# A fused attention and feed-forward kernel: the hand-written issue order runs on to step 27, and the last pair of f blocks is staged whole

## The chip, the core and the metric

The kernel runs on one core of a Trainium2 chip, in one launch. The time is device microseconds (us) of that core, the median of several executions. The engines named below are PE (TensorE: matmul, with its weight loads counted apart as PEld), DVE (VectorE), ACT (ScalarE), POOL (GpSimd) and SP (SyncE, which here only issues DMAs). Each engine has a list of instructions of its own, and in the trace they start in the order of that list.

## What is computed

```python
# q, k, v: (8, 8, 576, 64)   factor = 4
q_d, k_d, v_d = (a.reshape(B, H, S // 4, 4, D).mean(axis=3) for a in (q, k, v))
out_up = np.repeat(softmax_attn(q_d, k_d, v_d), 4, axis=2)      # down-sampled attention
scores = np.where(abs(pos[:, None] - pos[None, :]) < 4, scale * q @ k.T, -1e9)
out_local = softmax(scores) @ v                                 # band of 7 diagonals
x = (out_up + out_local).transpose(0, 2, 1, 3).reshape(4608, 512)
h = np.maximum(x @ w_in, 0)                                     # w_in 512 x 2048
out = (s * h * h + b) @ w_out                                   # w_out 2048 x 512
```

## The kernel before

**Feed-forward.** The 4608 tokens are cut into 18 blocks `t` of 256, the 2048 hidden features into 8 pairs `p` of 128-wide f blocks. One *step* is one (t, p). Its first product ("G", line 622, buffer `ph`) is 24 matmuls of 256 columns: x and w_in are each held as a high and a low part, and three of the four cross products are summed. ACT then does relu, square and a cast (`upper`, "R", lines 635 to 637, `gh`), DVE the low part `gl` (`lower`, "V", line 642). The second product ("H", lines 684 to 686, `po`) is 12 matmuls of 512 columns that sum over all p of a block; its first two thirds need `gh`, each third matmul needs `gl`. After p = 7 DVE scales the sum and adds the bias (line 696), and SP sends it out. The list `order` gives the steps: in both kernels the first 24 steps cover the blocks 0, 1 and 2 for all p, and step 24 is (3, 0).

**Weights.** The weights arrive as 64-bit floats. A pair's two halves (w_in part and w_out part) are loaded into a staging buffer (`load_w`, line 223), and `convert` (lines 247 to 257) makes the high and low parts: a chunk takes an ACT scaling, four DVE operations, an ACT cast and a DVE subtraction. Pairs 0 to 6 go through whole staging buffers of 1 MB a half. Pair 7 has no staging buffer: `load_quarter` (line 232) brings it in eight quarters of 256 columns through the two small buffers `pv`, and the same two buffers hold `convert`'s intermediate `es`.

**Bias.** The term b @ w_out is the column sum of w_out times b: `add_rows` adds 31 pieces on DVE (line 658), `column_sums` multiplies by ones on PE (line 662) and scales on DVE (line 663).

**Attention.** A unit is one batch and one pair of heads. Units 0 to 11 (batches 0 to 2) use a banded form in three streams: `d` (down-sampled: lines 315 to 375), `v` (values, POOL: lines 300 to 305) and `l` (the band: score products 431, sums 437 to 455, the diagonal blocks 459, output products `ol` 469, sum into x 473). Batches 3 to 7 use a form in which POOL and DVE make the band (lines 527 to 549) and PE only transposes the result (`ot`, line 559).

**What sets the order.** `PLAN` is a text of stream names: `d3` is the next piece of unit 3's d stream, `c5` the next piece of weight chunk 5, `x`/`y` the split of x for blocks 0, 1 and for block 2, `G R V H` the next piece of a step. Each piece is issued when its name comes up, and every PE, DVE, ACT and POOL instruction of it is tied behind the one before it on its engine. Before, `PLAN` holds units 0 to 7, pairs 0 to 6 and steps 0 to 14 (G) or 13 (H). What follows is written out by the loop at line 864 and placed by a scheduler: pair 7 (`split_w`), the bias sums, units 8 to 11, the evictions and steps 14 on. DMAs stand in SP's own queue in the order that the scheduler gives them.

Of the kernel before, what the change touches and what calls it, by code (L numbers as in the profile page):

```python
# [11 lines left out]
F32 = mybir.dt.float32  # L12
# [7 lines left out]
P = 128  # L20
# [57 lines left out]
def attention_ffn_kernel(ctx, tc, qk, vw_in, vr_in, vdm, qkn, vn, w_in, w_out, s_in, b_in, out):  # L78
# [55 lines left out]
    def load_pair(b, hp):  # L134
        if (b, hp) not in ld:
            load_parts(b, hp, ("qk", "vr", "vd") + (("vw",) if HP * b + hp < EU else ()))
# [81 lines left out]
    def load_w(p):  # L218

        parts = (("i", src_i[:, :, 512 * p : 512 * p + 512]), ("o", src_o[:, 2 * p : 2 * p + 2]))  # L220
        for op, src in parts:
            st = one.tile([P, 1024, 2], I32, tag=f"w{op}{STAGE[p]}", name="wst")
            nc.sync.dma_start(st.rearrange("p (k f) t -> p k (f t)", k=src.shape[1]), src)
            wst[(p, op)] = st

    def load_quarter(p, op, i):
        if op == "i":
            src = src_i[:, i, 512 * p : 512 * p + 512]
        else:
# [29 lines left out]
    def split_w(p):  # L259
        for chunk in split_parts(p):  # L260
            for _ in chunk:
                pass

    def split_parts(p):
        wi[p] = one.tile([P, 2, NK, 256], F32R, tag=f"wi{p}", name="wi")
        wo[p] = one.tile([P, 2, 2, DM], F32R, tag=f"wo{p}", name="wo")
        for op, w in (("i", wi[p]), ("o", wo[p])):
            fl = w.rearrange("p s k f -> p s (k f)")
            if p < len(STAGE):
                st = wst.pop((p, op))  # L270
# [672 lines left out]
```

## Time and profile before

| | |
|---|---|
| time, median of 3 runs | 965.31 us (965.13 to 965.32) |
| the profiled execution | 966.4 us, of which its instructions span 964.6 us |
| PE, PEld | 927.1 and 834.0 us busy, 96% and 86% of the span |
| DVE, ACT, POOL | 643.9, 479.1 and 404.3 us busy |
| DMA | 86.25 MB |

A matmul's bar in the trace also covers its way through the array, so bars of neighbours overlap: two bars of 0.28 us may start 0.12 us apart. A window of the trace ("A:B") gives, for each engine, the time in which at least one of its instructions ran. The chain of waits follows the work that ended last back to its start.

### The profile page before, as it was taken

Reading aid. Unit: us, or ns where it says so; the run is one execution under the profiler, and the core shown is the slowest. Engines: PE = TensorE matmul, PEld = TensorE weight load, DVE = VectorE, ACT = ScalarE, POOL = GpSimd, SP = SyncE. Lnnn points to the kernel's source line nnn. Section 1 sums busy time; section 2 is a strip of 40 time slices with the busy share of each in tenths; the row PEclk is TensorE's granted clock in tenths of the full one; section 3 lists DMA queues with packets and bytes.
Section 4 is the critical chain, followed back from the end, with each engine's and each line's share of the span. In section 5 each row is a group of like instructions: output and inputs, shape, how many; then the busy total and the mean of one; then the engine's idle time right before and its main releaser. Section 6 shows DMA issues by size and latency. Waiting matters only on the chain.

```text
span 964.6 us, 18495 instructions
## 1 busy us (share of the span) xinstructions
PE 927.1 (96%) x7316; PEld 834.0 (86%) x7316; DVE 643.9 (67%) x1154; ACT 479.1 (50%) x1141; POOL 404.3 (42%) x440
## 2 busy tenths in 40 slices
PE   5699999979999999999999999999999999999998
PEld 4589788768999999998898899999999999999997
DVE  7999978864577878787777878787878521111121
ACT  7877785454663454544353545454536333233231
POOL 5400220100176686768678777877676200000000
PEclk9799999999999999999999999999999999999999
DMA  9745321313143232322232424142412000000000
GB/s 326 255 162 182 120 87 41 98 60 107 58 138 110 79 125 79 125 75 91 79 119 66 138 66 138 67 138 66 138 54 76 1 22 1 24 1 22 1 23 22
DMA packets 32102, 86.25 MB, mean 89 GB/s; under 512 B 3344, under 2 KB 7952, under 8 KB 32016
## 3 DMA queue, kind: packets, MB, share of 16 engines
q1 hardware_dynamic: 32016, 85.08, 26.5%
q8 instruction: 57, 0.93, 0.4%
q14 instruction: 29, 0.24, 0.1%
HBM read 75.63 MB, written 9.44 MB: 88 GB/s over the span
## 4 chain that ended last, share of the span: by engine, by line
PE 72%; DVE 14%; POOL 4%; DMA 4%; issue 3%; ACT 2%; DVEq 0%; POOLq 0%; SPq 0%; ACTq 0%
PE ph L622 33%; PE po L684 11%; PE po L685 11%; PE po L686 11%; POOL pr L527 2%; POOL acc L549 2%; PE sa L334 2%; DMA tqk<-in_qk_dram 2%; DVE es L252 1%; DMA wst<-in_moe_w_out_dram 1%; DMA lqk<-in_qkn_dram 1%; DVE es L253 1%; PE sl L431 1%; PE up L375 1%; DVE st L529 1%
## 5 line engine op out<-in xcount | busy, mean ns | idle before, releaser
L622 PE MATMUL ph<-xh,wi 128*128 128x256 f32 x2176 | 409.6, 282 | 2.4 <-DVE gl L642 1.3
L622 PEld LDWEIGHTS ph<-xh,wi 128*128 128x128 f32 x2176 | 342.2, 189 | 9.8 <-DVE gb L642 2.3
L622 PE MATMUL ph<-xl,wi 128*128 128x256 f32 x1152 | 323.4, 281 | 1.0 <-DVE xl L744 1.0
L527 POOL TENSOR_TENSOR pr<-lqk 128x576 f32<-128x576 f32 x140 | 200.5, 1455 | 74.0 <-DMA lqk<-in_qkn_dram 37.6
L622 PEld LDWEIGHTS ph<-xl,wi 128*128 128x128 f32 x1152 | 217.0, 188 | 5.7 <-DVE xl L744 1.2
L635 ACT ACTIVATE ph<-ph 128x512 f32<-128x512 f32 x144 | 83.8, 582 | 230.3 <-PE ph L622 222.1
L684 PE MATMUL po<-wo,gh 128*128 128x512 f32 x456 | 181.4, 398 | 2.4 <-ACT gh L637 2.4
L685 PE MATMUL po<-wo,gh 128*128 128x512 f32 x456 | 180.8, 396 | 0.0
L686 PE MATMUL po<-wo,gl 128*128 128x512 f32 x456 | 177.5, 395 | 0.5 <-DVE gl L642 0.5
L642 DVE TENSOR_TENSOR gl<-ph,gh 128x512 fp32r<-128x512 f32 x114 | 78.0, 684 | 116.3 <-ACT gh L637 116.2
L549 POOL TENSOR_TENSOR acc<-acc,pv 128x576 f32<-128x576 f32 x80 | 114.9, 1436 | 55.0 <-DVE acc L549 29.4
L529 DVE TENSOR_REDUCE st<-pr 128x9 f32<-128x576 f32 x140 | 106.0, 757 | 38.1 <-POOL pr L527 35.6
L686 PEld LDWEIGHTS po<-wo,gl 128*128 128x128 f32 x456 | 85.8, 188 | 18.7 <-DVE gl L642 1.0
L684 PEld LDWEIGHTS po<-wo,gh 128*128 128x128 f32 x456 | 85.9, 188 | 18.5 <-ACT gh L637 3.2
L548 DVE TENSOR_TENSOR pv<-lv,st 128x576 f32<-128x576 f32 x120 | 87.6, 748 | 19.2 <-POOL acc L549 18.8
L685 PEld LDWEIGHTS po<-wo,gh 128*128 128x128 f32 x456 | 86.0, 189 | 14.8
L637 ACT CAST gh<-ph 128x512 fp32r<-128x512 f32 x114 | 66.9, 587 | 63.1 <-PE po L685 60.2
L636 ACT ACTIVATE ph<-ph 128x512 f32<-128x512 f32 x144 | 83.7, 582 | 3.4
L305 POOL TENSOR_TENSOR dq<-vq 64x64 f32<-64x64 f32 x58 | 19.6, 337 | 123.8 <-PE up L373 121.6
L304 POOL TENSOR_TENSOR dq<-vt 80x64 f32<-80x64 f32 x58 | 18.5, 330 | 88.9 <-PE up L375 87.1
L685 PE MATMUL po<-wo,gb 128*128 128x512 f32 x120 | 46.9, 391 | 0.0
L686 PE MATMUL po<-wo,gb 128*128 128x512 f32 x120 | 46.8, 390 | 0.0
(153 smaller groups left out, 1195.3 us busy)
## 6 DMA issues: line engine op xcount, KB each, us to landing
tqk<-in_qk_dram SPq DMA_DIRECT2D x30, 584.0 KB, 4.2
lqk<-in_qkn_dram SPq DMA_DIRECT2D x20, 768.0 KB, 4.2
lv<-in_vn_dram SPq DMA_DIRECT2D x20, 480.0 KB, 3.4
out_dram<-os SPq DMA_DIRECT2D x17, 512.0 KB, 3.1
wst<-in_moe_w_in_dram SPq DMA_DIRECT2D x7, 1024.0 KB, 5.4
wst<-in_moe_w_out_dram SPq DMA_DIRECT2D x7, 1024.0 KB, 5.2
tvd<-in_vdm_dram SPq DMA_DIRECT2D x29, 160.0 KB, 2.9
tvr<-in_vr_dram SPq DMA_DIRECT2D x29, 128.0 KB, 2.5
```

The lines of the kernel that those rows point to most:

```text
L527: nc.gpsimd.tensor_tensor(pr, lqk[:, 0:CH], lqk[:, CH + o : 2 * CH + o], ALU.mult)
L529: nc.vector.tensor_reduce(ls[:, :, o], pr, AX.X, ALU.add)
L548: nc.vector.tensor_tensor(pv, lv[:, o : o + CH], w, ALU.mult)
L549: (nc.vector if o % 3 == 1 else nc.gpsimd).tensor_tensor(acc[:, :, h], acc[:, :, h], pv, ALU.add)
L622: nc.tensor.matmul(ph[:, j], wi[p][:, s, k, f], xk[:, k], start=k == 0 and s == 0 and xk is xh, stop=k == NK - 1 and s == 1)
L635: nc.scalar.activation(ph, ph, AF.Relu)
L636: nc.scalar.activation(ph, ph, AF.Square)
L637: nc.scalar.copy(gh, ph)
L642: nc.vector.tensor_tensor(gl, acc.pop((t, p)), gh.bitcast(F32), ALU.subtract)
L684: nc.tensor.matmul(po[m], gh[:, j, ms], wo[p][:, 0, j], start=first, stop=False)
L685: nc.tensor.matmul(po[m], gh[:, j, ms], wo[p][:, 1, j], start=False, stop=False)
L686: nc.tensor.matmul(po[m], gl[:, j, ms], wo[p][:, 0, j], start=False, stop=last)
```

## The change

`PLAN` is rewritten from its first piece and now reaches through step 27. It holds units 0 to 11, all eight pairs, the bias sums (`b`, `s`), the evictions of blocks 0 and 1 (`E`), the split of x for block 3 (`z`), and, as names with `w` and `q`, the places of the loads of pairs 2 to 7 and of the attention inputs of the units 5 to 11.

Pair 7 is loaded in two whole halves, one after the other, into the memory of batch 2's x, which is free until unit 8 writes there, and converted in four chunks of 512 columns. The steps of blocks 0 and 1 for pair 7 move from places 21 and 22 to places 16 and 17. Blocks 0 and 1 are evicted through buffers of the tag `xh`, which hold the split x of blocks 0 and 1 before and of block 3 after. Units 8 to 11 use the banks 2 and 3 that the sums of block 1 leave, and G alternates between bank 4 and another.

```diff
 PLAN = (
-    "d0 l0 d1 l1 d1 d2 l2 d1 l1 d2 d3 d0 d2 d1 d3 l0 l1 d1 v2 d2 d0 d2 l1 l2 d1 l1 v1 l3 d1 "
+    "d0 d0 l1 d1 l0 l1 d1 d2 d1 d3 d2 l1 d1 d3 d0 v1 l1 l0 l1 d1 l1 l0 d0 d1 l1 l2 d1 l0 d0 "
...
-    def load_w(p):
-        parts = (("i", src_i[:, :, 512 * p : 512 * p + 512]), ("o", src_o[:, 2 * p : 2 * p + 2]))
...
-    def load_quarter(p, op, i):
...
+    def load_w(p, op):
+        if op == "i":
+            src = src_i[:, :, 512 * p : 512 * p + 512]
+        else:
+            src = src_o[:, 2 * p : 2 * p + 2]
+        if p < len(STAGE):
             st = one.tile([P, 1024, 2], I32, tag=f"w{op}{STAGE[p]}", name="wst")
+        else:
+            st = new_x(2).rearrange("p h s -> p (h s)")[:, 0:2048].bitcast(I32)
+            st = st.rearrange("p (f t) -> p f t", t=2)
...
+            n = 1024 if WIDE <= p < len(STAGE) else 512
+            for j in range(0, 1024, n):
+                js = slice(j, j + n)
+                yield convert(wst[p, op][:, js], fl[:, 0, js], fl[:, 1, js], op, p)
...
-        at = 6 if t >= 3 and p % 2 else 7 if t == 1 and p < HF else 4
+        at = 4 if order.index((t, p)) % 2 == 0 else 6 if t >= 3 and (t, p) != (3, 1) else 7 if t == 1 and p < HF else 5
...
+    def evict(t):
+        if t < 2:
+            os_ = two.tile([P, 2, DM], F32, tag="xh", name="os")
+        else:
+            os_ = one.tile([P, 2, DM], F32, tag="os", name="os")
...
+    def fourth_x():
+        xs[3] = xh, xl = tuple(
+            two.tile([P, HP, TB], F32R, tag=tag, name=tag) for tag in ("xh", "xl"))
...
-    order += [(2, p) for p in range(HF)]
-    order += [(t, p) for p in range(HF, NFP) for t in range(3)]
+    order += [(2, 0), (2, 1)] + [(t, HF) for t in range(2)]
+    order += [(2, p) for p in range(2, NFP)]
...
+    bk = {0: banks(*range(8)), 1: two_banks(5, 6), 2: two_banks(2, 3)}
...
+            for name in plan:
+                if name[0] in "wq":
+                    load(name)
+                    continue
+                if name not in streams:
+                    begin_stream(name)
                 next(streams[name], None)
...
-    begin = 2 * HF
+    begin = 28
```

On DVE the first step's `gl` (line 642 before, 637 now) stands after this piece of the order. `xl` is the low part of x, `es` and `wi` belong to the weight chunks, `sm`, `pl`, `qd`, `kd`, `dmx` to attention. Before:

```order
L744 TENSOR_TENSOR xl<-x,xh 128x256
L315 TENSOR_REDUCE qd<-tqk 128x144
L317 TENSOR_REDUCE kd<-tqk 128x144
L437 TENSOR_REDUCE sm<-sl_816 128x6
L438 TENSOR_TENSOR pl<-sl_816,sm 128x192
L257 TENSOR_TENSOR wi<-es,wi 128x512
L249 TENSOR_SCALAR es<-es 128x512
L250 TENSOR_SCALAR es<-es 128x512
L642 TENSOR_TENSOR gl<-ph,gh 128x512
```

Now, from the same split of x on:

```order
L747 TENSOR_TENSOR xl<-x,xh 128x256
L308 TENSOR_REDUCE qd<-tqk 128x144
L310 TENSOR_REDUCE kd<-tqk 128x144
L254 TENSOR_SCALAR es<-es 128x512
L255 TENSOR_SCALAR es<-es 128x512
L257 SCALAR_TENSOR_TENSOR es<-wst,es 128x512
L258 SCALAR_TENSOR_TENSOR es<-wst,es 128x512
L339 RECIPROCAL dsm<-dsm 96x3
L254 TENSOR_SCALAR es<-es 128x1024
L255 TENSOR_SCALAR es<-es 128x1024
L637 TENSOR_TENSOR gl<-ph,gh 128x512
```

More of the weight chunks stands ahead of the first `gl`, a wide chunk of pair 2 (128x1024) among it; in all DVE has 114 instructions ahead of it now, and 106 before.

SP's queue around pair 7 read so before (`wst` is a quarter of pair 7; `tqk`, `tvr`, `tvd`, `tvw` are a unit's inputs):

```order
L131 DMA tvw<-in_vw_dram 128x768
L232 DMA wst<-in_moe_w_in_dram 128x512 x2
L131 DMA tqk<-in_qk_dram 128x1168
L232 DMA wst<-in_moe_w_in_dram 128x512
L131 DMA tvr<-in_vr_dram 128x256
L232 DMA wst<-in_moe_w_out_dram 128x512
L131 DMA tvd<-in_vdm_dram 80x512
L131 DMA tvw<-in_vw_dram 128x768
L232 DMA wst<-in_moe_w_out_dram 128x512 x3
L131 DMA tqk<-in_qk_dram 128x1168
```

Now the two halves of pair 7 (`x`) stand with one unit input between them, and ahead of the outputs of blocks 0 and 1:

```order
L140 DMA tvw<-in_vw_dram 128x768
L140 DMA tvd<-in_vdm_dram 80x512
L140 DMA tvr<-in_vr_dram 128x256
L237 DMA x<-in_moe_w_in_dram 128x4x512
L140 DMA tvw<-in_vw_dram 128x768
L237 DMA x<-in_moe_w_out_dram 128x2x1024
L671 DMA out_dram<-os 128x2x512 x2
L140 DMA tqk<-in_qk_dram 128x1168 x2
```

The quarters are gone from between the inputs, and no attention input stands behind four of them any more.

On ACT the split of x for block 3 (`xh`) stood among pair 7's chunks before:

```order
L247 ACTIVATE es<-wst 128x256
L442 ACTIVATE pl<-pl 128x384
L365 COPY ptm<-tp 80x288
L635 ACTIVATE ph<-ph 128x512
L603 CAST xh<-x 128x1024
L255 CAST wo<-es 128x256
L636 ACTIVATE ph<-ph 128x512
L459 COPY db<-pt 32x12x32 x4
L368 COPY ptr<-tr 64x144 x2
```

Now it stands behind the R of step 18, in unit 8's d stream (`dq`, `dmx`, `pd`, `dsm`) and ahead of the R of step 19:

```order
L632 CAST gh<-ph 128x512
L315 COPY dq<-qd 64x3x48 x2
L765 CAST xh<-x 128x1024
L331 ACTIVATE dmx<-dmx 96x3
L333 ACTIVATE pd,dsm<-sa,dmx 96x144 x3
L337 ACTIVATE dsm<-dsm,eps 96x3
L630 ACTIVATE ph<-ph 128x512
L631 ACTIVATE ph<-ph 128x512
L632 CAST gh<-ph 128x512
L342 ACTIVATE pd<-pd,dsm 96x144 x3
```

Its memory is the buffer from which block 0 has just been sent out, so it also follows the end of that transfer.

More of the change, by code (lines that the diff above doesn't have):

```diff
@@ L435, in near @@
                 yield
+                if h == 0:
+                    pl = own["pl"] if own else two.tile([P, 2 * NG, 32], F32, tag="pl", name="pl")
+                    sm = own["sm"] if own else two.tile([P, 2, 2 * NG], F32, tag="sm", name="sm")
+                    lmx, lsm = sm[:, 0], sm[:, 1]
                 hg = slice(h * NG, h * NG + NG)
@@ L649, in gemm1, with add_rows @@
             lower(t, p)
-    def add_rows(p):
-        parts = [wo[p][:, i // 2, i % 2].bitcast(F32) for i in range(4)]
-        if p == 0:
-            nc.vector.tensor_tensor(bias, parts.pop(), parts.pop(), ALU.add)
-        for part in parts:
-            nc.vector.tensor_tensor(bias, bias, part, ALU.add)
+    def add_rows():
+        for p in range(NFP):
+            parts = [wo[p][:, i // 2, i % 2].bitcast(F32) for i in range(4)]
+            if p == 0:
+                nc.vector.tensor_tensor(bias, parts.pop(), parts.pop(), ALU.add)
+                yield
+            for part in parts:
+                nc.vector.tensor_tensor(bias, bias, part, ALU.add)
+                yield
     def column_sums():
@@ L662, in column_sums @@
         nc.tensor.matmul(cs, ones, bias, start=True, stop=True)
+        yield
         nc.vector.tensor_scalar(bias, cs, sb_b, None, ALU.mult)
+        yield
+    def evict(t):
[3 more added lines that the diff above has]
+            os_ = one.tile([P, 2, DM], F32, tag="os", name="os")
+        for i in range(2):
+            nc.vector.scalar_tensor_tensor(
+                os_[:, i], oacc[t][i], sb_s, bias, ALU.mult, ALU.add)
+        nc.sync.dma_start(
+            out[TB * t : TB * t + TB, :].rearrange("(m p) c -> p m c", p=P), os_)
     def gemm2(t, p):
@@ L677, in products2 @@
         end = t == NB - 1 and p == NFP - 1
-        os_ = one.tile([P, 2, DM], F32, tag="os", name="os") if p == NFP - 1 else None
+        os_ = one.tile([P, 2, DM], F32, tag="os", name="os") if end else None
         for m in range(2):
@@ L693, in products2 @@
                     nc.sync.dma_start(out[r0 : r0 + P, cs], os_[:, m, cs])
-            elif p == NFP - 1 and m == 1:
-                for i in range(2):
-                    nc.vector.scalar_tensor_tensor(
-                        os_[:, i], po[i], sb_s, bias, ALU.mult, ALU.add)
-                nc.sync.dma_start(
-                    out[TB * t : TB * t + TB, :].rearrange("(m p) c -> p m c", p=P), os_)
+            elif p == NFP - 1 and m == 1 and t >= 2:
+                evict(t)
             yield
@@ L779, in attention_ffn_kernel, with two_banks @@
     offset_mask()
[L781 to L797 removed]
+    at = {"sa": 0, "tp": 0, "up": 0, "tr": 1, "sl0": 1, "sl1": 0, "ol": 1}
+    def two_banks(*ids):
+        return lambda shape, name: bank(ids[at[name]], shape, name)
+    bk = {0: banks(*range(8)), 1: two_banks(5, 6), 2: two_banks(2, 3)}
+    chunks = (chunk for p in range(NFP) for chunk in split_parts(p))
+    streams = {"x": begin_x(), "y": third_x(), "z": fourth_x(), "b": add_rows()}
+    streams["s"] = column_sums()
+    streams["E"] = (evict(t) for t in range(2))
     streams["G"] = (None for t, p in order for _ in products1(t, p))
@@ L801, in attention_ffn_kernel, with begin_stream, load @@
     streams["H"] = (None for t, p in order for _ in products2(t, p))
+    def begin_stream(name):
+        if name[0] == "c":
+            streams[name] = next(chunks)
+            return
+        b, hp = units[int(name[1:])]
+        for kind, steps in banded(b, hp, bk[b]).items():
+            streams[f"{kind}{HP * b + hp}"] = steps
+    def load(name):
+        if name[0] == "w":
+            load_w(int(name[1]), name[2])
+        else:
+            load_parts(*units[int(name[1:-1])], {"k": ("qk",), "v": ("vr", "vd"), "w": ("vw",)}[name[-1]])
     plan = PLAN.split()
@@ L832, in attention_ffn_kernel @@
     free = [0, 0, 16] + [((S * (b - 1) - 1) // TB) * NFP - 2 for b in range(3, B)]
-    rings = {1: banks(5, 6), 2: banks(5), 3: banks(2, 3, 5)}
+    ring = banks(2, 3, 5)
+    part_done = [i for i in range(2 * HP, EU) if f"d{i}" in streams]
     def attention_rest():
-        for i in range(2 * HP, EU):
+        for i in part_done:
+            b, hp = units[i]
+            load_pair(b, hp)
+            d, v, l = (streams[f"{kind}{i}"] for kind in "dvl")
+            next(v, None)
+            for _ in itertools.chain(d, l):
+                yield
+        for i in range(part_done[-1] + 1, EU):
             load_ahead(i)
-            yield from first_unit(*units[i], rings[min(i // HP + i // (EU - 2), 3)])
+            yield from first_unit(*units[i], ring)
         for b, g in GROUPS:
-            yield from two_pairs(b, g, rings[3])
+            yield from two_pairs(b, g, ring)
     gen = attention_rest()
-    done = NY[1]
+    done = NY[1] + NY[2] * len(part_done) // HP
     pend = []
```

72 lines of the change are left out of this document (17 added, 55 removed), and 35 rows, old and new, of the table PLAN.

## The prediction, made before the run

> **What bounds the kernel now.** I read the page's busy line, then windows of the trace, then the chain of waits in the one window that shows a loss.
>
> ```profile
> PE 927.1 (96%) x7316; PEld 834.0 (86%) x7316; DVE 643.9 (67%) x1154; ACT 479.1 (50%) x1141; POOL 404.3 (42%) x440
> 0.00:56.54 56.54, 36.02 (x663) 30.82 (x663) 50.53 (x106) 44.54 (x119) 24.80 (x60) 0.85 0.76 260
> 56.54:128.00 71.46, 68.72 (x775) 59.92 (x775) 69.73 (x106) 54.70 (x109) 7.25 (x12) 1.00 0.47 154
> 128.00:175.44 47.44, 46.97 (x425) 40.53 (x426) 37.78 (x72) 29.49 (x75) 4.67 (x12) 1.00 0.22 72
> 175.44:229.69 54.25, 46.95 (x445) 39.11 (x445) 34.90 (x75) 25.70 (x61) 5.75 (x12) 0.97 0.19 62
> 229.69:300.00 70.31, 70.31 (x647) 64.25 (x648) 43.95 (x81) 42.27 (x114) 30.39 (x40) 1.00 0.34 117
> 543.70:964.60 420.90, 417.11 (x2745) 380.27 (x2745) 214.43 (x375) 169.80 (x380) 159.85 (x151) 1.00 0.16 54
> ```
>
> The columns are length, then busy time of PE, PEld, DVE, ACT and POOL, granted clock, DMA share, GB/s. PE bounds the whole after 229.69, where step 24 begins: it is busy without a hole, so only what delays PE before that moves the end. DVE bounds the front: between the first `gl` at 56.54 and the eleventh at 128.00 it runs 69.73 of 71.46 us. From 128 on PE leads again, and from 175.44 (first H of the 18th step, counted 17 from 0) to 229.69 both PE and DVE have holes.
>
> Those 54.25 us hold PEld 39.11. Where PE never waits, PEld fills 64.25 of 70.31 (0.914) or 380.27 of 420.90 (0.903). The same work without waits takes 39.11/0.914 = 42.8 to 39.11/0.903 = 43.3, so **11.2 us** are lost there (10.9 to 11.5). PE's own holes give less, 54.25 - 46.95 = 7.3, since the last bar ahead of each hole is drawn to its modelled end.
> The Trainium skill (Perfetto Trace Analysis, Identifying the Most-Contended Engine) says that matmul busy time is no good measure of headroom, and that the busy share of the weight loads is. By the first reading the loss is 7.3, by the second 11.2; this trace bears out the second, since the stretches without holes hold one PEld share within 1.2%.
>
> What makes the loss, from the chain of waits and the list of waits between 160 and 230:
>
> ```profile
> 177.15 2.76 DMA wst<-in_moe_w_in_dram
> 184.54 2.92 DMA wst<-in_moe_w_out_dram
> 189.85 2.50 DMA wst<-in_moe_w_out_dram
> 195.90 2.96 DMA wst<-in_moe_w_out_dram
> 201.16 3.10 DMA wst<-in_moe_w_out_dram
> ...
> ACT es L247 <- DMA wst<-in_moe_w_out_dram: 7.8, 4, 2.8
> ACT es L247 <- DMA wst<-in_moe_w_in_dram: 4.0, 3, 2.0
> PE up L373 <- ACT ptr L368: 3.7, 1, 3.7
> ```
>
> Five quarters of pair 7 follow one another, each issued only when a chunk has freed a `pv` buffer. ACT stands 11.8 us at their doors with the casts of R and the copies for attention queued behind, and PE at last waits 3.7 us for `ptr`. Granted clock is 0.97 here against 1.00 around, 0.03 x 54.25 = 1.6 us worth of clock, after that hole.
> The Trainium skill (TensorE: Matmul & The Clock Gate, Part 1) says that an idle window of some 3.4 us halves the clock; the one hole of 3.75 us with the lower clock behind it agrees. By that rule the holes that I forecast below, 2 us and less, cost no clock; if they did, each would cost some 1.6 us more.
>
> **The change, part by part.**
>
> *Taken away:* the quarter loads, so the 11.2 us, if nothing takes their place. Whatever DVE has more ahead can be late next.
>
> *The front.* In the new order PE, where it comes to the second product of step 17, has done the same 204 H matmuls as before at 175.44, 456 G matmuls instead of 432, and less score work: two sets of 48 `sl` bars, six `sa`, three `tp`.
>
> ```profile
> 643.10 2.83 PE ph L622 x24
> 58.96 0.62 PE L431 MATMUL sl<-tqk 64*32 64x32 f32 x48
> ```
>
> That is +2.8 - 1.2 - 0.7 - 0.4 = +0.5 us (the last two from 0.12 us a matmul as in the first row): level. But that H needs `gl` of step 17, and DVE has more ahead of it.
>
> ```profile
> 0.00:128.00 128.00, 104.74 (x1438) 90.74 (x1438) 120.26 (x211) 99.24 (x227) 32.05 (x72) 0.93 0.60 201
> 0.00:177.14 177.14, 153.11 (x1870) 132.18 (x1870) 159.74 (x286) 128.94 (x302) 36.72 (x84) 0.95 0.49 164
> L658 DVE TENSOR_TENSOR bias<-bias,wo 128x512 f32<-128x512 f32 x30 | 21.6, 720 | 0.2
> L249 DVE TENSOR_SCALAR es<-es 128x512 f32<-128x512 f32 x8 | 3.2, 401 | 0.0
> L250 DVE TENSOR_SCALAR es<-es 128x512 int32<-128x512 int32 x8 | 4.9, 611 | 0.3
> L252 DVE SCALAR_TENSOR_TENSOR es<-wst,es 128x512 int32<-128x512 int32 x8 | 5.7, 718 | 0.1
> L253 DVE SCALAR_TENSOR_TENSOR es<-wst,es 128x512 int32<-128x512 int32 x8 | 5.5, 692 | 0.3
> L257 DVE TENSOR_TENSOR wi<-es,wi 128x512 fp32r<-128x512 f32 x4 | 2.9, 736 | 0.0
> L249 DVE TENSOR_SCALAR es<-es 128x256 f32<-128x256 f32 x8 | 2.3, 293 | 4.2 <-ACT es L247 4.2
> L250 DVE TENSOR_SCALAR es<-es 128x256 int32<-128x256 int32 x8 | 2.3, 289 | 0.1
> L252 DVE SCALAR_TENSOR_TENSOR es<-wst,es 128x256 int32<-128x256 int32 x8 | 3.5, 436 | 0.1
> L253 DVE SCALAR_TENSOR_TENSOR es<-wst,es 128x256 int32<-128x256 int32 x8 | 3.6, 454 | 0.1
> L257 DVE TENSOR_TENSOR wi<-es,wi 128x256 fp32r<-128x256 f32 x4 | 1.7, 420 | 0.3 <-ACT wi L255 0.2
> L315 DVE TENSOR_REDUCE qd<-tqk 128x144 f32<-128x576 f32 x29 | 21.7, 748 | 15.9 <-DMA tqk<-in_qk_dram 15.9
> ```
>
> Counted in the order lists up to that `gl`: seven bias sums more (7 x 0.72 = 5.0); four chunks of 512 columns (4 x 3.16 = 12.6) for three of 256 less two last subtractions still to come (3 x 1.47 + 2 x 0.42 = 5.3); five reductions of q and k fewer (5 x 0.75 = 3.7) and nine small score operations (about 0.33 each, 3.0). 5.0 + 12.6 - 5.3 - 3.7 - 3.0 = **+5.6 us**. DVE then needs 159.7 + 5.6 = 165.3 us of work. How long it stands idle ahead of that no row shows. The lower bound is what it stood by the eleventh `gl`, 128.00 - 120.26 = 7.7; the upper is before's whole 177.14 - 159.74 = 17.4, much of it waiting for PE. I take 9.5, near the row of the stretch that DVE bounds, since the new order gives DVE more to do while PE's share stands level. So `gl` starts at 174.8, ends 0.7 later, and is needed two matmuls (0.46) after H begins: H begins as if at 175.1, against 175.44. At the front **nothing is won or lost** (-1.8 with 7.7, +7.9 with 17.4).
>
> *Behind it* PE has 43.0 - 0.5 = 42.5 us of work up to before's state at 229.69, so it gets there at 217.6: **12.1 us earlier**, if it does not wait anew.
>
> *New waits.* The rows for the transfers:
>
> ```profile
> out_dram<-os SPq DMA_DIRECT2D x17, 512.0 KB, 3.1
> wst<-in_moe_w_in_dram SPq DMA_DIRECT2D x7, 1024.0 KB, 5.4
> wst<-in_moe_w_out_dram SPq DMA_DIRECT2D x7, 1024.0 KB, 5.2
> tvw<-in_vw_dram SPq DMA_DIRECT2D x9, 384.0 KB, 3.2
> L696 DVE SCALAR_TENSOR_TENSOR os<-po,sb_s,bias 128x512 f32<-128x512 f32 x34 | 25.1, 746 | 9.4 <-PE po L686 7.0 <-DMA out_dram<-os 2.4
> ```
>
> (1) `tvw` has one buffer. Between the last `ol` of unit 10 and the first of unit 11 PE has only 12 G matmuls, an `up` and 6 H matmuls, 1.4 + 0.4 + 1.4 = 3.2 us; likewise between units 8 and 9, nearer 2.8. A load that is issued when the one ends lands 3.2 later, plus about 0.4 for the two semaphores: 0.6 twice, **1.2** (0 to 6.4). Behind `ol` all of PE is queued. (2) The split of x for block 3 goes into the buffer that block 0 leaves through: two DVE operations (1.5), then 3.1 for the transfer, and ACT waits, with unit 8's `pd` and the R of step 19 behind it. PE has two H halves and three G halves meanwhile, about 7 us, then wants `pd`: **2.0** (0 to 4.6, all bare). (3) The halves of pair 7: each waits for its buffer alone, w_in's for block 2's first split of x, w_out's for the last read of w_in's. Ahead of the first chunk stand three H halves, 4.1 us, against 5.4; ACT waits about 1, PE has the next G: **0.5** (0 to 10.6, both bare). Sum 3.7.
>
> *The rest at nothing.* The evictions of blocks 0 and 1 and the column sum only change place; G hides them, and uncovered they cost 4 x 0.75 = 3.0. The later batches start behind unit 11's last `ol`, which comes earlier too. There POOL is near:
>
> ```profile
> 268.88 9.74 POOL L527 TENSOR_TENSOR pr<-lqk 128x576 f32<-128x576 f32 x7 [4.09 <-DMA lqk<-in_qkn_dram]
> L559 PE MATMUL ot<-ident,acc x90: 270/273/329, 323.7 to 767.3; 128*128 128x128 f32 x90
> PE ot L559 <- POOL acc L549: 1.6, 1, 1.6
> ```
>
> PE waits once, 1.6 us, for POOL in 500 us. The first `ot` stands 37 steps in instead of 39.5, the last `ol` at 27.5 instead of 29.1, so PE's cover shrinks by some 2 us; uncovered that is 2, and I cost 0.
>
> **Sum.** Against the profiled execution: 966.4 (964.6 span + 1.8 around it) - 12.1 + 3.7 = 958.0. That execution is 1.1 above the median shown, 965.31, so the forecast is 965.3 - 8.4 = **956.9 us**.
>
> **The rivals.**
> *All new waits are hidden and DVE idles only 7.7:* 965.3 - 12.1 - 1.8 = 951.4, more likely 953. For it: each wait is within 2 us of its cover. Against: three places, each in an in-order queue.
> *DVE stands idle as long as before (17.4):* the front costs 7.9 and eats the gain, 956.9 + 7.9 = 964.8. For it: 114 instructions instead of 106 stand ahead of the first `gl`. Against: before's idle time came from step 12 on, when PE led.
> *Only PE's holes are won* (7.3, not 11.2): 960.8.
> *Slower:* both halves of pair 7 lie bare at ACT's head (the first and third new chunk), since SP issues them late: w_out's stands behind a `tvw`, which waits for unit 7's last `ol`. Price 5.4 + 5.2 - 0.5 = 10.1 above the forecast, 967.0, and with block 0's transfer bare as well (4.6 for 2.0) 969.6. The gain is gone from a bare wait of 8.4 us on. For it: the trace's quarters did just this, 11.8 us. Against: each half now waits for its buffer once, not for four chunks.
>
> **How the numbers follow.** The forecast (954.5 to 962) has 0.5, the first rival 0.18, DVE's idling 0.16, PE's holes only 0.06, slower 0.10. The range of 8 in 10 reaches from the first rival's likelier end, 951.5, to beyond the second, 966. What a measurement tells from no change is 0.2%, 1.9 us: faster is under 963.4. The forecast, the first and the third rival lie there but for a few hundredths, and a quarter of the second: 0.77. Same 0.12, slower 0.11.
>
> **What would show it.** Right: no PE hole over 2.5 us between 175 and 215 and clock 1.00 there; step 24 begins near 221; DVE over 95% busy from 60 to 170; short waits of PE `ol` on DMA `tvw`, and of ACT's `xh` on `out_dram`. Wrong: DVE idle over 12 us by step 17's `gl`; ACT waiting over 4 us for a half of pair 7; PE waiting for `ot` at the first group; or a first `gl` later than 63.

## The result and the profile after

| kernel | median of the runs, us | range | ratio to the kernel before (95%) |
|---|---|---|---|
| before | 965.32 | 965.13 to 965.32, and one execution of 2340.94 that the ratios leave out | 1 |
| changed | 956.87 | 956.12 to 957.84 | 0.9914 (0.9894 to 0.9933) |
| changed, run again beside the second group of experiments | 957.04 | 956.26 to 959.19 | 0.9895 (0.9873 to 0.9916) |

The changed kernel is faster by 8.4 us, 0.9%. Beside the three groups of experiments below, the kernel before ran again, with medians of 965.91, 967.17 and 966.44 us, so the ratio to before in the same group stands beside each time. The profiled execution spans 956.0 us where that of before spans 964.6.

First the busy line and the chain's shares by engine, from the page of the changed kernel:

```profile
PE 928.4 (97%) x7316; PEld 835.7 (87%) x7316; DVE 639.5 (67%) x1134; ACT 476.8 (50%) x1133; POOL 416.2 (44%) x440
...
PE 84%; DVE 7%; DMA 3%; POOL 2%; ACT 1%; issue 1%; SPq 0%; DVEq 0%; POOLq 0%
```

PE's share of the chain that ended last is 84%, and was 72% before. Then the same kind of windows as were shown of before (length, then busy time of PE, PEld, DVE, ACT and POOL, granted clock, DMA share, GB/s). They are cut at the first `gl` (57.30), at 128, at the first H of step 17 (174.06) and at the start of step 24 (223.80):

```profile
0.00:57.30 57.30, 40.84 (x714) 35.44 (x714) 54.00 (x115) 47.88 (x128) 27.19 (x60) 0.82 0.80 273
57.30:128.00 70.70, 69.25 (x760) 60.81 (x759) 66.71 (x102) 55.05 (x115) 10.28 (x18) 1.00 0.46 150
128.00:174.06 46.06, 45.40 (x311) 39.80 (x309) 43.32 (x72) 24.84 (x46) 3.88 (x7) 1.00 0.24 77
174.06:223.80 49.74, 48.69 (x641) 41.25 (x639) 31.01 (x62) 27.77 (x77) 4.67 (x12) 1.00 0.26 87
223.80:300.00 76.20, 74.05 (x589) 66.70 (x586) 51.02 (x90) 39.52 (x102) 42.62 (x46) 1.00 0.31 103
0.00:174.75 174.75, 156.11 (x1782) 136.24 (x1782) 164.73 (x287) 128.36 (x290) 41.35 (x84) 0.94 0.51 171
```

The stretch from step 17 to step 24 is where the kernels differ: 49.74 us with 1.05 us of holes in PE's bars, against 54.25 with 7.3, and the clock is 1.00 there. DVE is now nearly full up to 174 (43.32 of 46.06 us between 128 and 174.06, where before it had 37.78 of 47.44). And a hole that before did not have stands behind step 24: 2.15 us between 223.80 and 300.

Step 24 starts 5.9 us earlier, with less work left as well, since the new order had done more by then. The groups of PE's matmuls from there to the end, of before and then of the changed kernel, show how much (only the groups whose counts differ; `sl` is the score of the near part):

```profile
L685 PE MATMUL po<-wo,gh 128*128 128x512 f32 x362 | 143.1, 395 | 0.0
L684 PE MATMUL po<-wo,gh 128*128 128x512 f32 x362 | 142.7, 394 | 0.0
L686 PE MATMUL po<-wo,gl 128*128 128x512 f32 x364 | 142.0, 394 | 0.0
L334 PE MATMUL sa<-kd,dq 128*96 128x144 f32 x132 | 21.3, 286 | 0.0
L431 PE MATMUL sl<-tqk 64*32 64x32 f32 x144 | 1.9, 196 | 0.0
```

```profile
L692 PE MATMUL po<-wo,gh 128*128 128x512 f32 x360 | 142.4, 396 | 0.0
L691 PE MATMUL po<-wo,gh 128*128 128x512 f32 x360 | 142.1, 395 | 2.0 <-DVE os L669 1.7 <-ACT gh L632 0.3
L693 PE MATMUL po<-wo,gl 128*128 128x512 f32 x360 | 141.0, 393 | 0.0
L327 PE MATMUL sa<-kd,dq 128*96 128x144 f32 x126 | 20.6, 286 | 0.0
L421 PE MATMUL sl<-tqk 64*32 64x32 f32 x52 | 0.8, 196 | 0.0
```

Eight H matmuls (0.23 us from one to the next), six `sa` (0.12), 92 small `sl` (0.013, from the 0.62 us of 48) and the two passes of the column sum (0.46) make 4.2 us. So the changed kernel is 5.9 + 4.2 = 10.1 us ahead at step 24, and 8.6 at the end of the span: some 1.5 are lost again behind it. The second fence shows most of it: PE waits 1.7 us for `os`, once.

The new waits of the changed kernel are, for PE, in two rows of its timeline (start, length, the wait ahead of it in brackets):

```profile
176.94 1.10 PE L658 MATMUL cs<-bias,ones 128*128 128x512 f32 x2 [0.93 <-DVE bias L653]
291.02 0.50 PE L691 MATMUL po<-wo,gh 128*128 128x512 f32 x1 [1.72 <-DVE os L669]
```

For ACT they are in the list of waits between 100 and 260 and between 145 and 176 (engine, line and what it waited for, total, times, longest):

```profile
ACT xh L765 <- DMA out_dram<-os: 5.6, 1, 5.6
ACT es L252 <- DMA x<-in_moe_w_in_dram: 3.8, 1, 3.8
ACT es L252 <- DMA x<-in_moe_w_out_dram: 1.2, 1, 1.2
```

ACT waits longer than forecast in the places that the forecast named. One of these waits reaches PE, by way of DVE. ACT's 3.8 us for w_in's half end at 149.31; DVE then stands idle for the chunk that ACT has still to scale, is full from there on, and is late with a `gl` for which PE waits:

```profile
150.00 0.43 DVE L254 TENSOR_SCALAR es<-es 128x512 f32<-128x512 f32 x1 [1.02 <-ACT es L252]
157.53 0.50 PE L693 MATMUL po<-wo,gl 128*128 128x512 f32 x1 [0.66 <-DVE gl L637]
```

In the profile of the changed kernel run again, DVE's idle time there is 1.6 us and PE's wait 1.2. PE also waits in two places that the forecast had at nothing. The experiments are about what won the time, and which of these waits cost any.

### The profile page after: what moved, and what is told of

It reads as the page before. It is cut to its first block, busy times and chain, and to the rows that moved or that the text cites. A ratio compares the mean times of both kernels' runs of the same rounds, so it can differ in the third digit from the quotient of the medians.

```text
span 956.0 us, 18449 instructions
## 1 busy us (share of the span) xinstructions
PE 928.4 (97%) x7316; PEld 835.7 (87%) x7316; DVE 639.5 (67%) x1134; ACT 476.8 (50%) x1133; POOL 416.2 (44%) x440
## 4 chain that ended last, share of the span: by engine, by line
PE 84%; DVE 7%; DMA 3%; POOL 2%; ACT 1%; issue 1%; SPq 0%; DVEq 0%; POOLq 0%
PE ph L617 38%; PE po L691 13%; PE po L692 13%; PE po L693 12%; PE sa L327 2%; PE ol L464 1%; PE up L368 1%; POOL pr L522 1%; DMA tqk<-in_qk_dram 1%; PE ot L554 1%; DMA wst<-in_moe_w_in_dram 1%; DMA tvd<-in_vdm_dram 1%; PE up L366 1%; PE sl L421 1%; DVE es L257 1%
## 5 line engine op out<-in xcount | busy, mean ns | idle before, releaser
L544 POOL TENSOR_TENSOR acc<-acc,pv 128x576 f32<-128x576 f32 x80 | 121.0, 1512 | 48.8 <-DVE acc L544 25.9
L524 DVE TENSOR_REDUCE st<-pr 128x9 f32<-128x576 f32 x140 | 105.9, 757 | 31.7 <-POOL pr L522 28.2
L297 POOL TENSOR_TENSOR dq<-vt 80x64 f32<-80x64 f32 x58 | 22.6, 401 | 174.5 <-PE up L368 172.9
L692 PE MATMUL po<-wo,gb 128*128 128x512 f32 x120 | 47.8, 398 | 0.0
L691 PE MATMUL po<-wo,gb 128*128 128x512 f32 x120 | 47.1, 392 | 0.0
L693 PE MATMUL po<-wo,gb 128*128 128x512 f32 x120 | 46.8, 392 | 0.0
```

The lines of the kernel that those rows point to most:

```text
L524: nc.vector.tensor_reduce(ls[:, :, o], pr, AX.X, ALU.add)
L544: (nc.vector if o % 3 == 1 else nc.gpsimd).tensor_tensor(acc[:, :, h], acc[:, :, h], pv, ALU.add)
L691: nc.tensor.matmul(po[m], gh[:, j, ms], wo[p][:, 0, j], start=first, stop=False)
L692: nc.tensor.matmul(po[m], gh[:, j, ms], wo[p][:, 1, j], start=False, stop=False)
L693: nc.tensor.matmul(po[m], gl[:, j, ms], wo[p][:, 0, j], start=False, stop=last)
```

## The experiments

The theory on record (A): eight quarter loads of pair 7, one behind another, made the stall in front of step 24, and staging pair 7 whole took it away. The rival (B): the new order won the time, and the staging only went along. The first two runs undo one half of the change each. The others take up the new waits.

### Pair 7 in quarters again, within the new order

```diff
-    "d7 V G d7 c17 l7 ... y V H y b w7i l7 b R H q8w b "
-    "l7 b H y ... G R b w7o c18 G c19 b b R V b H "
+    "d7 V G d7 c17 l7 ... y V H y b l7 b R H q8w b "
+    "l7 b H y ... G R b c18 G c19 b b R V b H "
...
+        st = two.tile([P, 256, 2], I32, tag="pv", name="wst")
+        nc.sync.dma_start(st.rearrange("p f t -> p (f t)"), src)
...
+                f = new_x(2).rearrange("p h s -> p (h s)")[:, at : at + 256]
...
-                yield convert(wst[p, op][:, js], fl[:, 0, js], fl[:, 1, js], op, p)
+                if p == NFP - 1:
+                    yield two_quarters(fl, op, p, j // 256)
+                else:
+                    yield convert(wst[p, op][:, js], fl[:, 0, js], fl[:, 1, js], op, p)
```

`two_quarters` loads two quarters through `pv` and converts them in the place of one chunk of 512 columns. The intermediate `es` lies in batch 2's x here and not in `pv`, so both `pv` buffers are free for loads: the last two quarters of w_in are issued 0.8 us apart, where before the third and fourth went out 9 us apart. So these quarters are not quite those of before.

> The changed kernel, with pair 7 staged in eight quarters through pv as before, in the same place of the new plan. Theory A (the quarters made the stall, and staging pair 7 whole took it away): the stall comes back. ACT waits at the quarters' loads for some 8 to 12 us again, PE loses 6 to 11 us of it between steps 17 and 24, and the time goes back to 962 to 968. Theory B (the new order of the rows made the gain, staging only went along): time 955 to 959, and what ACT waits at the quarters is hidden from PE.

Measured: 962.33 us, ratio 0.9963 (0.9950 to 0.9976). The quarters cost 5.3 to 5.5 us in the new order. From the list of waits between 150 and 176:

```profile
PE po L721 <- DVE gl L665: 3.4, 1, 3.4
ACT x L277 <- DMA wst<-in_moe_w_out_dram: 4.1, 3, 1.9
ACT x L277 <- DMA wst<-in_moe_w_in_dram: 2.4, 2, 1.6
```

ACT waits 6.5 us at the loads, less than the 8 to 12 forecast, and PE feels it through DVE: `gl` stands in DVE's queue behind a quarter's operations, which wait for ACT, which waits for the load. PE waits these 3.4 us in one piece, at 161.33, and the granted clock is 0.91 from 160 to 180 (1.00 in the changed kernel), worth 1.8 us. The loss stands in front of step 17, not between steps 17 and 24 as theory A had it, since the new order has pair 7 earlier. The time is at the low edge of A, but 3.6 us of the gain (965.91 - 962.33) stay without the staging, which A does not explain.

### Pair 7 whole, within the old order

```diff
-                for i in range(4):
-                    cs = slice(256 * i, 256 * i + 256)
-                    yield convert(load_quarter(p, op, i), fl[:, 0, cs], fl[:, 1, cs], op, p)
+                st = new_x(2).rearrange("p h s -> p (h s)")[:, 0:2048].bitcast(I32)
+                st = st.rearrange("p (f t) -> p f t", t=2)
+                src = (src_i[:, :, 512 * p : 512 * p + 512] if op == "i" else src_o[:, 2 * p : 2 * p + 2])
+                nc.sync.dma_start(st.rearrange("p (k f) t -> p k (f t)", k=src.shape[1]), src)
+                for j in range(0, 1024, 512):
+                    js = slice(j, j + 512)
+                    yield convert(st[:, js], fl[:, 0, js], fl[:, 1, js], op, p)
```

> The kernel before, its order table untouched, with pair 7 alone staged whole in the memory of batch 2's x. Theory A (staging is the gain): 954 to 960, the stall of 11 us between steps 17 and 24 shrinks to under 3 us. Theory B (the order is the gain): 963 to 967; the waits at the quarters go, but PE waits for something else in the same place, since the attention rows and H of that stretch still stand in the old order.

Measured: 970.68 us, ratio 1.0046 (1.0025 to 1.0066): slower than before. Neither theory allowed that. In the timeline the load of w_out's half is issued at 164.26, when w_in's half has been read, and lands 6.4 us later; these are ACT's rows of the timeline, and PE's next wait (L639 to L641 are the three operations of R, L247 the first of a chunk):

```profile
168.15 0.58 ACT L639 ACTIVATE ph<-ph 128x512 f32<-128x512 f32 x1 [1.60 <-PE ph L626]
170.76 1.22 ACT L247 ACTIVATE es<-x 128x512 f32<-128x512 f32 x2 [2.03 <-DMA x<-in_moe_w_out_dram]
171.88 0.59 ACT L640 ACTIVATE ph<-ph 128x512 f32<-128x512 f32 x1
...
173.14 0.58 PE L688 MATMUL po<-wo,gh 128*128 128x512 f32 x1 [2.54 <-ACT gh L641]
```

The chunk stands between the first and the second operation of an R, so the load's wait goes straight into `gh` and into PE. By the first G of step 17 this kernel is 4.6 us behind the one before (175.10 against 170.46).

By step 24 it is only 1.6 behind (231.30 against 229.69), since the later quarters' waits are gone. One wait of the old stall is not gone:

```profile
213.39 0.48 PE L377 MATMUL up<-ptr,dq 128*128 128x144 f32 x2 [2.60 <-ACT ptr L372]
```

Before, PE waited 3.7 us for `ptr`. Here no load is in front of it: ACT works without a hole from 208.74 on at the first operation of an R, the cast of x, two copies `db`, the second operation of the R and two more `db`, and `ptr` comes behind them. Behind both of these waits the granted clock is lower (0.91 from 160 to 180 and from 200 to 220). The rest of the loss lies behind step 24 and is not taken apart.

In the order of the changed kernel w_out's half is issued at 154.40, ACT waits 1.2 us for it, and each R stands in one piece between the chunks. So staging without the order wins nothing here (4.8 us lost), the order without staging wins 3.6, and both together 8.4. Neither A nor B holds alone: the gain is that of the pair. Two limits stay: pair 7 lies in the part of the program that the scheduler places, so the place of the halves in this run is the scheduler's choice, and another place within the old order was not tried. The whole halves want a place in ACT's queue where little that PE needs stands behind them.

### The split of x for block 3 off the output transfer

```diff
-            os_ = two.tile([P, 2, DM], F32, tag="xh", name="os")
+            os_ = two.tile([P, 2, DM], F32, tag=("xh", "xl")[t], name="os")
```

> The changed kernel, with block 1's output evicted through the buffer of xl instead of xh, so that the split of x for block 3 no longer follows block 0's output transfer at once. ACT's wait of 5.6 us at that transfer should shrink to under 2. By the prediction's term (2.0 us of it reach PE): 955 against 957. By the trace of the changed kernel (PE stands level across it, so it is covered by H and G halves): 956.5 to 957.5, no change.

Measured: 957.71 us, ratio 0.9912 (0.9895 to 0.9928), no change. ACT's 5.6 us at the transfer are gone from its list of waits between 100 and 260, and another stands in their place:

```profile
ACT dmx L331 <- DVE dmx L329: 8.3, 2, 5.9
```

The next instruction in ACT's queue (`dmx` of unit 8) had to wait that long anyhow (0.3 us behind the transfer before). The transfer's wait cost nothing.

### Without the row sums on DVE

```diff
-                nc.vector.tensor_tensor(bias, bias, part, ALU.add)
+                pass
```

> The changed kernel without 30 of the 31 additions that sum the rows of w_out on DVE (the output's bias then lacks them), 21.6 us of DVE's work gone. Theory C (DVE is the engine that the first 18 steps wait for, and the sums also delay the column sum, for which PE stands 2.2 us): the time falls by 2.2 to 6 us, 951 to 954.7, and PE's wait at the column sum is gone. Rival (PE bounds the front too, and what is won is lost again where DVE waits for POOL behind step 30): 956 to 957.5.

Measured: 953.29 us, ratio 0.9873 (0.9856 to 0.9891), 3.6 us below the changed kernel. Busy times between 60 and 170, of the changed kernel and of this one:

```profile
60.00:170.00 110.00, 108.26 (x1039) 95.67 (x1038) 103.45 (x161) 77.40 (x156) 14.16 (x24) 1.00 0.40 129
```

```profile
60.00:170.00 110.00, 109.27 (x1049) 97.11 (x1048) 92.39 (x143) 77.20 (x156) 14.04 (x24) 1.00 0.39 129
```

With 21.6 us of DVE's work gone, PE gains 1.0 us in that stretch, and it does not wait at the column sum. By the 3.6 us that 21.6 us less of DVE's work win, PE and DVE bound this front together, within some 4 us of each other, and what PE gains in front of step 24 does reach the end. The rival falls.

### The column sum one H half later

```diff
-    "b b H b b H V b H R b b d8 s H s d8 V G E H E G d8 l8 z d8 H l8 d8 d9 G d8 R d8 z l8 l9 "
+    "b b H b b H V b H R b b d8 H s s d8 V G E H E G d8 l8 z d8 H l8 d8 d9 G d8 R d8 z l8 l9 "
```

> The changed kernel with the column sum's matmul one H half later in the order table (behind the second half of step 17's product instead of ahead of it). PE's wait of 0.93 us for DVE's last row sum, and the 2.2 us that PE loses there between steps 18 and 19, should be gone or under 0.8. Theory (what PE loses in front of step 24 reaches the end): 1.4 to 2.2 less than the changed kernel, ratio to the kernel before some 0.989. Rival (POOL and DVE set the time behind step 30, so it is taken back there): no difference, 0.991.

Measured: 956.88 us, ratio 0.9888 (0.9867 to 0.9909), beside 0.9895 for the changed kernel in the same group: no change. The matmul no longer waits; the next does, for the bank that the column sum holds until DVE has read it:

```profile
179.96 0.39 PE L617 MATMUL ph<-os,wi 128*128 128x256 f32 x1 [0.84 <-DVE bias L660]
```

The rival's time is right, its reason is not: nothing is taken back behind step 30. DVE is late at this point of the program, and PE meets that one matmul further on.

### Block 3 out of PSUM by ACT

```diff
+            if t == 3:
+                nc.scalar.activation(os_[:, i], oacc[t][i], AF.Copy, scale=sb_s)
+                nc.vector.tensor_tensor(os_[:, i], os_[:, i], bias, ALU.add)
+                continue
             nc.vector.scalar_tensor_tensor(
                 os_[:, i], oacc[t][i], sb_s, bias, ALU.mult, ALU.add)
...
-                evict(t)
+                with tc.high_priority():
+                    evict(t)
```

The second part also lets the scheduler place the evictions of all later blocks sooner.

> The changed kernel with block 3's output taken out of PSUM by ACT (scaled copy) and only its bias added on DVE, so that the banks come free without standing in DVE's queue behind the reductions that wait for POOL. PE's wait of 1.7 us (2.0 us lost between steps 34 and 35) should go. Theory (it reaches the end): 1.5 to 2.0 less than the changed kernel. Rival (POOL's chain of products delays PE there in another place, at the next ot or the next H): under 0.5 less, the loss stands at steps 36 to 70 instead.

Measured: 958.27 us, ratio 0.9902 (0.9882 to 0.9923), not faster. The wait has moved, not gone:

```profile
290.42 0.21 ACT L531 ACTIVATE st<-st 128x63 f32<-128x63 f32 x1 [1.96 <-DVE st L530]
...
291.64 0.68 ACT L670 ACTIVATE os<-po,sb_s 128x512 f32<-128x512 f32 x1
...
292.37 0.50 PE L695 MATMUL po<-wo,gh 128*128 128x512 f32 x1 [2.06 <-ACT os L670]
```

The exponential of the local chain (L531) stands ahead of the copy in ACT's queue and waits for the same reductions on DVE, so this run does not separate the theories. The granted clock is 0.91 from 280 to 300 here (1.00 in the changed kernel), which is 1.8 us more.

### The changed kernel again

Beside the column sum, ACT's eviction and the sums on POOL, as the measure for these three.

> The changed kernel as it is, beside the others on the same chip: 956 to 958, ratio 0.990 to 0.993.

Measured: 957.04 us, ratio 0.9895 (0.9873 to 0.9916), as in the first comparison (0.9914).

### The row sums on POOL

```diff
-                nc.vector.tensor_tensor(bias, bias, part, ALU.add)
+                nc.gpsimd.tensor_tensor(bias, bias, part, ALU.add)
```

> The changed kernel with the 30 later additions of the row sums on POOL instead of DVE, in the same places of the order table. POOL is idle in most of that stretch, but takes some 1.3 us for each (1.46 us for 128x576 in the trace), about 39 us against DVE's 21.6. If POOL keeps up, the time is that of the kernel without these sums, 953 to 954 (DVE bounds the front). If it does not, PE waits longer for the column sum than the 2.2 us of now, 5 to 10 us, and the time is 958 to 965.

Measured: 967.87 us, ratio 1.0009 (0.9994 to 1.0024), beyond both cases: the whole gain of the change is lost. POOL takes 1.46 us for each sum and does not keep up (26 of them from 143.30 to 183.60), and DVE does not get faster with 21.6 us less to do. PE's largest wait is not for the column sum, as expected, but for a `gh` (4.4 us). Why is shown in the last section.

### Fewer row sums, taken earlier

```diff
         nc.vector.tensor_tensor(lo, f, hi.bitcast(F32), ALU.subtract)
+        if op == "o" and p >= 5:
+            for c in range(0, n, DM):
+                nc.vector.tensor_tensor(bias, bias, f[:, c : c + DM], ALU.add)
...
-        for p in range(NFP):
+        for p in range(5):
             parts = [wo[p][:, i // 2, i % 2].bitcast(F32) for i in range(4)]
```

> The changed kernel with the row sums of pairs 5, 6 and 7 taken from the unsplit half es right behind its split (two additions a pair instead of four, hi and lo being the parts of es): 6 of the 31 additions fewer on DVE, 4.3 us, all of them in the last 25 us ahead of the column sum. Theory (DVE is late at the column sum by some 2 us, and what PE loses in front of step 24 reaches the end): PE's loss of 2.2 us between steps 18 and 19 shrinks to under 0.7, the time is 1.5 to 3 us under the changed kernel's, 954 to 955.5, ratio 0.987 to 0.989. Rival (a PE wait for another engine takes its place there, as with the column sum one step later): 956 to 957.5.

Measured: 958.41 us, ratio 0.9917 (0.9901 to 0.9932): no gain. The wait at the column sum is gone, as forecast, and two others stand ahead of it:

```profile
158.31 0.50 PE L694 MATMUL po<-wo,gh 128*128 128x512 f32 x1 [0.92 <-ACT gh L635]
160.41 0.80 PE L696 MATMUL po<-wo,gl 128*128 128x512 f32 x1 [1.36 <-DVE gl L640]
```

The sums that are left of pairs 5 to 7 now stand right behind their chunk. Those of pair 6 thereby stand ahead of a `gl` and of block 2's first split of x, for whose end the load of w_in's half for pair 7 waits:

```profile
142.12 1.96 DVE L265 TENSOR_TENSOR bias<-bias,es 128x512 f32<-128x512 f32 x2
...
152.18 1.23 ACT L252 ACTIVATE es<-x 128x512 f32<-128x512 f32 x2 [5.21 <-DMA x<-in_moe_w_in_dram]
```

The load is issued at 145.68 and not at 143.34, ACT waits 5.2 us for it instead of 3.8, and the R and the `gl` behind it are late. The profiled execution is one of the longer ones (960.85), with a granted clock of 0.97 from 60 to 170, so the two waits may be longer in it than in the others. On a full engine it counts not only how many instructions there are but which one they stand ahead of.

### Block 3's eviction ahead of the local chain

```diff
-            elif p == NFP - 1 and m == 1 and t >= 2:
-                evict(t)
+            elif p == NFP - 1 and t >= 2:
+                if m == 0:
+                    oe = one.tile([P, 2, DM], F32, tag="os", name="os")
+                nc.vector.scalar_tensor_tensor(oe[:, m], po[m], sb_s, bias, ALU.mult, ALU.add)
+                if t == 3:
+                    ahead[m] = traced_last()
...
                 nc.vector.tensor_reduce(ls[:, :, o], pr, AX.X, ALU.add)
+                stands_behind(0)
...
             nc.vector.tensor_tensor(ls, ls, omask, ALU.add)
+            stands_behind(1)
```

`stands_behind(m)` puts that instruction behind half m's eviction in DVE's order. The edit also evicts the halves of the other blocks from 2 to 16 each by itself, without holding them anywhere.

> The changed kernel with block 3's two halves evicted each by itself, and held on DVE ahead of the last reduction (first half) and of the mask (second half) of the local chain, where they stood behind both before. PE's wait of 1.7 us for os between steps 34 and 35 should shrink to under 0.7. Theory (it reaches the end): 1 to 2 us less, 955 to 956. Rivals: the local chain that is held up by 0.7 to 1.5 us makes PE wait for ot later, or what follows is ordered anew by the scheduler and loses as much: 956.5 to 958.

Measured: 954.56 us (954.13 to 955.31), ratio 0.9871 (0.9857 to 0.9886): 2.3 us below the changed kernel and faster than both. Its runs lie clear of the changed kernel's (956.12 and up). The changed kernel was not run in this group, and the interval overlaps that of its second ratio (0.9873 to 0.9916). Within the group, "Fewer row sums, taken earlier" and "Both at once" differ by this edit alone, and by 2.2 us (958.41 and 956.21). DVE's rows there in the changed kernel, and then in this one (L524 and L537 are the reductions, L669 and L719 the eviction):

```profile
287.84 0.76 DVE L524 TENSOR_REDUCE st<-pr 128x9 f32<-128x576 f32 x1 [0.63 <-POOL pr L522]
...
290.28 0.69 DVE L669 SCALAR_TENSOR_TENSOR os<-po,sb_s,bias 128x512 f32<-128x512 f32 x1
```

```profile
289.29 0.75 DVE L719 SCALAR_TENSOR_TENSOR os<-po,sb_s,bias 128x512 f32<-128x512 f32 x1 [1.31 <-PE po L708]
289.95 0.75 DVE L537 TENSOR_REDUCE st<-pr 128x9 f32<-128x576 f32 x1
290.61 0.74 DVE L719 SCALAR_TENSOR_TENSOR os<-po,sb_s,bias 128x512 f32<-128x512 f32 x1
```

DVE now waits for PE there, and PE's next H begins at 290.09 without a wait in its row. Between 225 and the end PE's list of waits holds 0.6 us in all, where the changed kernel's two profiles hold 3.5 and 2.8, of which 1.7 are this wait in both. So the wait's 1.7 us reached the end. The rest of the 2.3 is not taken apart: it may come from later rows that the scheduler sets anew, or from the other blocks' evictions.

### Both at once

The two last diffs together.

> Both edits together, the six additions fewer and the earlier eviction of block 3. If both losses reach the end: 953 to 954.5, ratio 0.985 to 0.988. If only the first does: 954 to 955.5; if neither: 956.5 to 958.

Measured: 956.21 us, ratio 0.9892 (0.9880 to 0.9905). The first edit costs in this run what it cost alone, and the second wins: the sum is near the changed kernel. The better version is the one with the eviction alone.

## Why the prediction was right, and where only its sum was

The forecast was 956.9, the result is 956.87. That the two agree so closely is luck: the direction, the stall and the front were worked out rightly, but the waits that were priced and those that were not cancel.

| term, us | forecast | measured | by |
|---|---|---|---|
| `gl` of step 17 starts | 174.8 | 174.06 | DVE's row, windows |
| DVE's work and idle time ahead of it | 165.3 and 9.5 | 164.0 and 10.0 | window to 174.75, less its 0.68 |
| PE waits for `tvw` | 1.2 | 0 | PE's list of waits |
| block 0's output ahead of the split | 2.0 | 0 | run with the other buffer |
| halves of pair 7 | 0.5 | 0.7 to 1.2 | PE's wait for `gl`, two profiles |
| column sum | 0 | about 2.0 | PE's rows, run without the sums |
| block 3's eviction behind POOL's chain | 0 | 1.7 | run with the eviction ahead |

**The stall.** It was sized well. PE is 1.9 us ahead at step 17 (175.44 - 174.06, and the 0.5 us of work that the prediction counted) and 10.1 at step 24. So 8.2 are won between, although 2.0 are lost anew at the column sum: the old loss was some 10.2 us. That is near the 11.2 that PEld's share gave, and not the 7.3 of PE's own holes. The Trainium skill's rule on the busy share of the weight loads (Perfetto Trace Analysis, Identifying the Most-Contended Engine) is borne out by the 8.2 + 2.0. About 1 us stays unexplained.

**Its cause was put too simply.** "Taken away: the quarter loads, so the 11.2 us, if nothing takes their place." In the old order something does take their place: w_out's half, bare at ACT's head between two operations of an R. That is the mechanism of the slower rival, which the forecast gave 0.10, and it was kept out by the order, not by the staging. Besides, the 3.7 us for `ptr`, which the prediction laid to the quarters, are still 2.6 without them, because of the casts and copies that ACT has ahead of `ptr`. PE's list between 160 and 230 of before also held 2.4 us for `gh` and 1.2 for `gl`, which the prediction did not show. In the new order the quarters, with more buffers, cost 5.4 us, not 11.2. The time was right because the change made both at once.

**The front** went as worked out, within 1 us: DVE's added work and its idle time are both within 1.3 us of the forecast, and from 145 to 176 PE waited once for another engine, 0.7 us for the `gl` that w_in's half made late. (Of the three chunks of 256, two last subtractions were done by then and one was to come; the prediction's numbers have it so, its words the other way round.) DVE is 94% busy from 60 to 170 (103.45 of 110), where "over 95%" had been named as a sign.

**The new waits.** Of the three that were priced, the first two (1.2 and 2.0) cost PE nothing. For `tvw`, the 0.4 us for two semaphores stand in no row: in the kernel before, a `tvw` load is issued 0.04 us after the last `ol` (147.19), and ACT starts 0.08 after a quarter has landed (179.91). The split of x was priced on ACT and then carried on to PE by the cover that PE's own next rows give. What this left out is what ACT's next instruction waits for anyhow: 5.9 us for `dmx` behind a transfer of 5.6. The third, the halves, cost about what was forecast, but by another way: not through ACT into PE's next G, but through DVE into a `gl`. From that hole to the column sum DVE has no other, so its 1.0 us may also be part of what is lost there; no run takes it away alone. The two waits that cost most were in the part called "the rest at nothing". The column sum was priced as uncovered work (3.0 at most), but its cost is a wait: DVE's last row sum is late. These are PE's rows from the first H half of step 17 to the first G of step 19:

```profile
174.06 0.39 PE L691 MATMUL po<-wo,gh 128*128 128x512 f32 x1
...
174.80 0.51 PE L693 MATMUL po<-wo,gl 128*128 128x512 f32 x1
...
179.25 0.28 PE L617 MATMUL ph<-os,wi 128*128 128x256 f32 x1
```

From 174.06 to 179.25 are 5.2 us, for twelve H matmuls (2.8) and two passes of the column sum (0.46): 2.0 are lost, 0.3 of them for `gl`. The eviction of block 3 was not in the forecast at all. POOL was seen to be near in that place, but only `ot` was followed, not DVE's queue, in which the eviction stands behind reductions that wait for POOL.

**The signs named.** No hole over 2.5 us and clock 1.00 between 175 and 215: so it was. Step 24 near 221: 223.8, with 4.2 us less left to do, as 219.6 would have been in before's order. DVE over 95% busy: nearly. Short waits of `ol` on `tvw`: none; the wait of `xh` on `out_dram` came, but of 5.6 us. Of the signs that would have shown it wrong none came clearly: DVE was idle 10.0 us by `gl` of step 17 (12 was the limit), ACT waited 3.8 at most for a half (4 was the limit; 4.3 in the profile of the second run), PE never waited for `ot`, and the first `gl` came at 57.3 (63).

**The rivals.** "All new waits hidden", 951.4 or 953, had two of the three named waits right and lost to the two unnamed ones. DVE did not idle for 17.4 us. The bare halves came about only in the old order.

The sum, then: 12.1 for the stretch, 1.0 more at the front (175.1 against 174.06), less 2.0 and 2.0 for the column sum and the eviction with what hangs on it, is 9.1; with the old loss at 10.2 instead of 11.2 it is 8.1. Measured in the span are 8.6. The wait for the half lies in front of step 17 and is in the 174.06.

## What to carry to other kernels

A load that blocks an in-order queue is cured by its place in that queue as much as by its size: move it to where nobody queued behind it is awaited, and test the two halves of such a change apart. When a wait is priced, follow the waiting engine's own next instruction: where that must wait as long for something else, the wait is free (ACT's 5.6 us here); where a full engine takes its input from it, the wait comes out elsewhere (ACT's 3.8 us, in a `gl`). And look for evictions that stand behind another engine's chain: the edit that moved one pair of them ahead won 2.3 us here, 1.7 of them in the wait itself.

## What the runs showed of the hardware

A POOL addition that runs beside DVE doubles DVE's time and more, for some of its operations only. Groups of DVE's instructions between 143 and 184, of the changed kernel and then of the kernel with the row sums on POOL (busy time, mean ns of one):

```profile
L258 DVE SCALAR_TENSOR_TENSOR es<-x,es 128x512 int32<-128x512 int32 x4 | 2.8, 692 | 0.1
L255 DVE TENSOR_SCALAR es<-es 128x512 int32<-128x512 int32 x4 | 1.7, 426 | 0.1
L262 DVE TENSOR_TENSOR wi<-es,wi 128x512 fp32r<-128x512 f32 x2 | 1.4, 683 | 0.0
L637 DVE TENSOR_TENSOR gl<-ph,gh 128x512 fp32r<-128x512 f32 x6 | 4.1, 682 | 0.0
```

```profile
L258 DVE SCALAR_TENSOR_TENSOR es<-x,es 128x512 int32<-128x512 int32 x4 | 6.6, 1646 | 0.1
L255 DVE TENSOR_SCALAR es<-es 128x512 int32<-128x512 int32 x4 | 5.6, 1398 | 0.1
L262 DVE TENSOR_TENSOR wi<-es,wi 128x512 fp32r<-128x512 f32 x2 | 2.9, 1454 | 0.0
L637 DVE TENSOR_TENSOR gl<-ph,gh 128x512 fp32r<-128x512 f32 x5 | 3.4, 679 | 0.0
```

Operations whose operands all lie in SBUF go from 692 to 1646, 426 to 1398 and 683 to 1454 ns; `gl`, which reads one operand from PSUM, stays at 679. The one with a single tensor input loses as much as those with two (972 ns). The Trainium skill (SBUF — State Buffer, SBUF: two separate sides) says that DVE and GpSimd share a pair of ports under an exclusive lock, which a DVE operation with two SBUF inputs or in a two-port mode contends for. These rows agree with it, and the added 0.8 to 1.0 us is most of one POOL addition (1.46 us). Work moved from a full DVE to an idle POOL was no relief for that reason: DVE was busy 34.60 us of that kernel's 40.3 us from 143.3 to 183.6 with 29 instructions, and 36.98 with 61 in the changed kernel.

The prediction priced its holes by the Trainium skill's idle window of some 3.4 us, behind which the clock halves (TensorE: Matmul & The Clock Gate, Part 1). In the profiled executions here the clock fell behind shorter holes. Behind PE's holes of 2.54 and 2.60 us in the run with pair 7 whole in the old order, and of 2.06 us in the run with block 3 out of PSUM by ACT, the granted clock was 0.91 over 20 us, which is 1.8 us each time. Behind the 1.72 us of the changed kernel it was 1.00. Where page and runs differ, the measurement decides: a hole of some 2 us could cost nearly as much again in clock.
